# A new order for the second two thirds of a transformer block, and row-pass hops on four engines

## The chip, the cores and the metric

The kernel runs on one core of a Trainium2 chip. A core has five engines, each with its own instruction queue that it works off in order: TensorE (matmuls; PE in the profile, PEld for its weight loads), VectorE (DVE), ScalarE (ACT), GpSimd (POOL) and SyncE (SP, which here issues most DMAs). Engines wait for each other through semaphores. The metric is the time of one execution on the device in microseconds; lower is better.

## The reference

One block of a transformer with adaptive layer normalization, for 2048 tokens of width 448 (inputs and output bfloat16):

```python
mod = (silu(c) @ w_mod).reshape(1, 6, 1, 448)          # sa, ca, ga, sb, cb, gb
h = layernorm(x) * (1 + ca) + sa
x = x + ga * A(h, wqkv, wo)      # 16 heads of 28; each token attends to itself and
                                 # 7 tokens at steps of 2 behind it; softmax; @ wo
h = layernorm(x) * (1 + cb) + sb
x = x + gb * B(h, w1, b1, w2, b2)  # layernorm once more, @ w1 (448x1792) + b1, gelu (tanh), @ w2 + b2
```

## The kernel before

Even and odd tokens don't attend to each other, so the tokens are held as two sequences of 1024, and every tile carries both. The front (layer normalization, transposition, q, k and v) and the output side run in 8 tiles p = 0 to 7 of 128 positions of both sequences; attention runs in 9 batches i = 0 to 8 of 114 positions; the MLP runs in 4 tiles t = 0 to 3 of 256 positions. ScalarE's tables divide the whole into phases: attention batches 0 to 4, MLP tile 0, batches 5 and 6, tile 1, batches 7 and 8, tiles 2 and 3; a table load (`tbl`) stands between exp and gelu.

A batch is: v (`v5f`, `v5r`: a matmul over 128 rows and a rest over 64), the logits in two halves (`lt`, line 781), exp on ScalarE (line 788), the mask on VectorE (line 794), the sums `pd` (line 803) and the weighted values `po` (line 814), log and exp of the sums on ScalarE (lines 823 and 825), and their product on VectorE (`omul`, line 831). Then, for a tile, `wo` (line 851, or in two passes at line 575), and on VectorE the residual sum (`x1`, line 860), statistics (line 459), a normalization (line 481), two products with the modulation (`h2`, line 869), statistics and a normalization again, and the copy of a tail of 64 columns (lines 493 to 495); `rstd` between them is on GpSimd (line 472). A transposing DMA of SyncE (`yT`, line 884) brings the result into the layout for w1. An MLP tile is w1 (seven pairs of column blocks, line 575), 14 gelus on ScalarE (line 914), w2 (line 938, for the last tile line 956), and the residual sum (`fin`, line 962), which reads x plus a bias that GpSimd makes beforehand (`x1p`, line 891; a tiny copy `gate`, line 918, holds it back until the first gelu). The weights w2 are multiplied by a gate vector on VectorE (`w2_scale`, line 704, seven of them), after their loads (line 378). `windows` (lines 731 and 732) copies columns for v.

Where a matmul's inner dimension is cut to 64 rows, two of them run side by side in the upper and the lower half of the array, and write into two PSUM areas. In a first pass each half adds its share to its own area, in a second pass the halves change areas. The second pass must not begin before the first has ended, so between them stands a *hop*: an instruction on another engine that waits for the last matmul of the first pass and on which the first matmul of the second pass waits. `swapped` adds the hop, `paired` uses it for w1, for wo of tiles 4 to 7 and for v of batch 8, and the MLP uses it for w2 of tiles 0 to 6; there are 40. In TensorE's order other work stands between the two passes of a pair (`...p` and `...q`; for w2 `..._l` and `..._h`).

Nothing is scheduled at run time. The program makes a list of 781 tasks (`add`), each with an engine, an estimate of its time, a function that emits its instructions, and, for some, alternatives on other engines (`alt`). `ORDER` is the list of task numbers in which they are emitted; a letter behind a number picks an alternative (A ScalarE, D VectorE, P GpSimd, R another form on TensorE). An engine's queue is what stands in `ORDER` for it, in that order. `SLOTS` gives each buffer its place (PSUM has four of two banks); a task that writes a new buffer into a place waits for the last user of the one before. Both were written by a search outside the kernel.

Task numbers that are used below: 182 and 179 are the scalings of w2's blocks 4 and 1, 178, 183, 184 others of them; 352 and 385 are the omul of batches 3 and 4, 353 (`wo2`) and 386 (`wo3`) the output projections that need them; 463 and 500 are v of batches 5 and 6; 268 is yT0; 472, 473 and 509, 510 are pd and po of batches 5 and 6; 477, 479 and 514, 516 are the passes of wo4 and wo5, 515 the hop between the last two; 547, 549, 550 and 569 are passes of w1 in tile 1; 579 is the hop of w2 for tile 2; 535 and 498 are yT5 and yT4; 668 is the first task of w1 in tile 2; 629 is a copy of windows, 371 and 497 are tails.

Of the kernel before, what the change touches and what calls it, by code (L numbers as in the profile page):

```python
# [50 lines left out]
]  # L51
ORDER = """
3 14 17 0 1 15 5 9 10 18 11 16 13 19 20 2 6 24 21 73 55+12@55 26 12 71 25 56 72 74 57 75 22 58 77 23 59 60 27 62 61 76
32 4 67 66 68+11@68 78 63 28 108 64 30 110 69 79 84:A 89:P 31 65 70 109 111 80 88:P 83 34 81 112:P 87:A 29 101+9@101
85 90:A 93:P 36 114 94+3@94 82 95 113 102 92:A 91 115:D 86 103 116 96 120:A 144 97 99 104 106 117:A 135 98 118:A 142
105 119:A 145 143 133 100 146 121 136 134 137 126 148 107 147 149:D 127 7 138 122 150 124 129 139 190 198 123 191 200
140 128 141 199 269 125 236 271 130 270 207 40 209 33 241 237 201 38 208 210 185 211 35 242 39 202 154 153 151:A 152
187 8 238 239 212 159 203 213 186 204 214:D 155 240 205 215 188 278 156 279 280 160 206 307:R 161 281 243 282 272 192
273:A 37 157 189 171 162 308:D 194 172 193 283 244 218 163 195 219 275 173 284 196 216 167 158 285 217 246 462:P 197
164 286 168 165 228 169:D 174 274 276:D 309 277 312 220 313 166 310 314 221 229 225 230 224 311 222:D 247 315 170 245  # L60
176 317 316 175 248 233 226 232 290 318 227 249 289:A 319 287:A 43 288 320 234 250 223 592:P 593 46 321 45 253 345 47
342 346 251 594 231 303 499:P 252 324 343 322 291 44 254 595 323 325 347 326 344 292 304 255 327 293 348 328 373:R 256
305 294 329 257 350 258 375 378 52 330 376 340:R 53 333 379 235 377 334 331 374 296 300 295 332 259 41 335 351 380 299
336 341 49 337 260 297 382 262 381 301 263 261 349 264 338:A 352 463 383 339 265 384 353 266 267:D 406 385 268 500 354
# [8 lines left out]
580 598 635 532 533 638 636 581 534:D 639 535 602 582 588 498 604 605 641 640 603 642 587 606 643 607 667 589 678 608
644 668 609 669 583 679 670 610 645 613 680 646 611 681 684 612 614 615 685 647 682 590 674 683 648 703 691 686 649
687 671 650 617 675 651 698 672 616 692 460 618 673 453 619 688 652 622 677 653 620 676 693 689 699 655 623 690 654
696 621 656 700 624 694 657 708 705 695 701 658 697 715 660 702 659 661 662 709 663 664 625 665:A 626 716 710 666 627
# [26 lines left out]
class Plan:  # L103
# [53 lines left out]
def kernel(  # L157
# [14 lines left out]
    nc = tc.nc  # L172
# [3 lines left out]
    P = Plan()  # L176
    add = P.add
# [368 lines left out]
    def swapped(first, bufs, second):  # L546

        ends = []

        def hop():  # L550
            nop = nc.sync.nop()
# [484 lines left out]
```

## Time and profile before

| | |
|---|---|
| time, median of 3 runs | 171.2 us (170.81 to 173.26) |
| the profiled execution, as timed | 171.57 us |
| its span, first to last instruction | 169.9 us |
| mean granted TensorE clock | 0.998 |
| DMA | 18.84 MB, mean 111 GB/s |

The page gives the busy time of each engine and the costliest groups of instructions. A timeline row has the start in us from the span's start, the length in us, the engine, the line, the operation, out<-in with their shapes, the count, and in brackets idle time of the engine just before with what ended it. Successive matmuls overlap, so a row's length holds some 0.16 us of the last matmul's end, and a distance from start to start is the better measure. A row of stretches has the bounds and length in us, then the busy time of TensorE, its weight loads, VectorE, ScalarE and GpSimd with the count of instructions, the granted clock, the share of DMA time and GB/s. SPq is SyncE issuing a DMA; the landing comes later.

### The profile page before, as it was taken

The numbers are of one execution on the slowest core, as the hardware profiler recorded it, in microseconds if no ns is written. First come the engines' busy times: TensorE is split into PE (matmuls) and PEld (weight loads), VectorE is DVE, ScalarE is ACT, GpSimd is POOL, SyncE is SP. The second block draws the span as 40 slices with busy tenths as digits, with TensorE's granted clock in tenths as the row PEclk, the third lists the DMA queues.
The fourth block names the chain that finished last, engine by engine and source line by source line (L and its number), as shares of the span: only waits on it lengthen the run. The fifth ranks groups of instructions, "written<-read, shape, count | busy, mean of one in ns | idle before, by whom it ended". The sixth has DMA issues, their size and how long they took to land.

```text
span 169.9 us, 5815 instructions
## 1 busy us (share of the span) xinstructions
PE 160.9 (95%) x2528; PEld 86.8 (51%) x2528; DVE 118.3 (70%) x273; ACT 102.7 (60%) x142; POOL 47.1 (28%) x71
## 2 busy tenths in 40 slices
PE   7999999988999899999999999999799999999992
PEld 4678545444545544445555444556355555555650
DVE  6889799858899698698797459995559941300023
ACT  3378978697489944879447169948335920096300
POOL 3136422300351100391720014650010654007200
PEclk9999999999999999999999999999999999999999
DMA  5999989899999999910060000006013115100004
GB/s 155 319 355 293 193 242 158 168 127 173 227 183 262 174 136 256 139 30 4 8 121 4 4 0 0 4 4 123 5 58 123 39 21 106 54 4 0 0 17 149
DMA packets 35577, 18.84 MB, mean 111 GB/s; under 512 B 28507, under 2 KB 34592, under 8 KB 35552
## 3 DMA queue, kind: packets, MB, share of 16 engines
q1 hardware_dynamic: 35548, 18.47, 51.4%
q8 instruction: 20, 0.33, 0.9%
q14 instruction: 5, 0.04, 0.1%
q10 hardware_dynamic: 4, 0.00, 0.0%
HBM read 9.81 MB, written 1.84 MB: 69 GB/s over the span
## 4 chain that ended last, share of the span: by engine, by line
PE 64%; DMA 17%; DVE 10%; ACT 2%; POOL 2%; issue 2%; SPq 1%; DVEq 0%; POOLq 0%; ACTq 0%
PE p L575 25%; PE p L938 17%; DMA kT<-zy 6%; PE pw L851 4%; PE pq L591 4%; PE p L956 3%; PE pw L575 3%; DMA x_all<-in_A_x_dram 3%; DMA yT<-zy 3%; DVE stt L459 3%; DMA wm_st<-in_w_mod_dram 3%; DMA zT<-zy 2%; PE lt L781 2%; PE po L814 2%; POOL rs_all L472 1%
## 5 line engine op out<-in xcount | busy, mean ns | idle before, releaser
L914 ACT ACTIVATE hm<-p,b_col 128x512 bf16<-128x512 f32 x56 | 34.0, 692 | 28.1 <-PE p L575 28.1
L575 PE MATMUL p<-yT,w_s 64*128 64x512 bf16 x336 | 41.9, 376 | 1.1 <-DMA yT<-zy 1.1
L938 PE MATMUL p<-w_s,hm 64*128 64x448 bf16 x392 | 39.3, 350 | 0.0
L472 POOL TENSOR_TENSOR rs_all<-mvs,neg_half 128x2 f32<-128x2 f32 x22 | 16.9, 775 | 65.2 <-DVE mvs L461 65.0
L938 PEld LDWEIGHTS <-hm 64*128 64x128 bf16 x392 | 19.3, 94 | 16.4 <-issue 0.6
L575 PEld LDWEIGHTS <-w_s 64*128 64x128 bf16 x336 | 17.6, 94 | 19.4 <-issue 1.5
L962 DVE TENSOR_TENSOR x_all<-p,x1p 128x896 bf16<-128x896 f32 (+2 forms) x10 | 8.9, 900 | 24.2 <-PE p L956 16.6
L788 ACT ACTIVATE et<-lt 128x928 bf16<-128x928 f32 x18 | 16.2, 942 | 5.5 <-PE lt L781 5.3
L459 DVE BATCH_NORM_STATS2 stt<-x_all 128x6 f32<-128x448 bf16 x32 | 18.6, 611 | 0.8 <-DMA x_all<-in_A_x_dram 0.5
L891 POOL TENSOR_TENSOR x1p<-x_all,gbb_bc 128x448 f32<-128x448 bf16 x16 | 17.5, 1116 | 0.1
L591 PE MATMUL pq<-wqk_st,hT 128*128 128x448 bf16 x72 | 15.2, 354 | 0.3 <-DVE hT L505 0.3
L860 DVE TENSOR_TENSOR x_all<-pw,x_all 128x896 bf16<-128x896 f32 x8 | 8.7, 1088 | 7.0 <-PE pw L575 6.6
L794 DVE TENSOR_TENSOR et<-et,mask 128x928 bf16<-128x928 bf16 x18 | 11.7, 668 | 2.1 <-ACT et L788 2.1
L831 DVE TENSOR_TENSOR qT<-po,den 128x912 bf16<-128x912 f32 x9 | 9.9, 1098 | 3.4 <-PE po L814 1.8
L823 ACT ACTIVATE den<-pd 128x928 f32<-128x928 f32 x9 | 8.5, 942 | 5.1 <-PE pd L803 3.2
L575 PE MATMUL p<-yT,w_r 64*128 64x512 bf16 x56 | 10.8, 376 | 0.0
L671 ACT CAST zy<-pq 128x896 bf16<-128x896 f32 x10 | 8.9, 911 | 3.0 <-PE pq L597 1.4
L591 PEld LDWEIGHTS <-hT 128*128 128x128 bf16 x72 | 6.4, 98 | 7.4 <-issue 1.6
L869 DVE TENSOR_TENSOR h<-h,mod_bc 128x896 bf16<-128x896 bf16 x16 | 9.7, 613 | 0.2
L825 ACT ACTIVATE den<-den,den_bias 128x928 f32<-128x928 f32 x9 | 9.6, 1072 | 0.2
L481 DVE TENSOR_SCALAR h<-x_all,mvs,rs_all 128x448 bf16<-128x448 bf16 x16 | 8.0, 529 | 2.3 <-POOL rs_all L472 2.2
L459 DVE BATCH_NORM_STATS2 stt<-h 128x6 f32<-128x448 bf16 x16 | 9.5, 613 | 0.1
(121 smaller groups left out, 202.6 us busy)
## 6 DMA issues: line engine op xcount, KB each, us to landing
w_s<-in_B_w_dram SPq DMA_DIRECT2D x7, 224.0 KB, 6.3
out_dram<-x_all SPq DMA_DIRECT2D x7, 224.0 KB, 2.0
x_all<-in_A_x_dram SPq DMA_DIRECT2D x3, 448.0 KB, 5.2
wmod<-in_w_mod_dram SPq DMA_DIRECT2D x3, 448.0 KB
w_s<-in_B_w_dram SPq DMA_DIRECT2D x3, 448.0 KB
wqk_st<-in_A_wqkv_dram SPq DMA_DIRECT2D x3, 225.0 KB, 4.3
wm_st<-in_w_mod_dram SPq DMA_DIRECT2D x1, 672.0 KB, 4.6
x_all<-in_A_x_dram SPq DMA_DIRECT2D x2, 224.0 KB
```

The source lines that it names most:

```text
L459: add("DVE", 0.53, lambda: nc.vector.bn_stats(out=stt[:, w, b, 0:6], in_=src()), reads=reads, bufs=bufs, after=early if w == b == 0 else ( ...
L472: ways = {"POOL": (0.55 + 0.17 * n, lambda: nc.gpsimd.tensor_tensor(out=r, in0=v, in1=neg_half[:, 0:n], op=ALU.pow))}
L575: mm = nc.tensor.matmul(out(), lhsT=lhs(kt, rows), rhs=rhs(kt, rows), start=start and kt == 0, stop=not start and kt == n - 1, tile_positi ...
L591: nc.tensor.matmul(out(), lhsT=lhs(kt, slice(0, 128)), rhs=rhs(kt, slice(0, 128)), start=first and kt == 0, stop=not first and kt == KT - 2)
L788: exps.append(add("ACT", 0.83, lambda half=half, lt=lt: nc.scalar.activation(out=et.t[:, 2 * half:2 * half + 2].rearrange("p r m c -> p r ...
L794: nc.vector.tensor_tensor(out=ev, in0=ev, in1=mask[:], op=ALU.mult)
L825: exps.append(add("ACT", 0.96, lambda: nc.scalar.activation(out=den.t[:], in_=den.t[:], func=ACT.Exp, scale=-1.0, bias=den_bias[:]), bufs= ...
L831: nc.vector.tensor_tensor(out=qT[:, :, LEAD + q00:LEAD + q00 + 2 * WQ], in0=po.t[:, :, 0:NS * 4 * WQ].rearrange("p j (m c) -> p m j c", c=WQ),
L869: add("DVE", 0.55, lambda vec=vec, op=op: nc.vector.tensor_tensor(out=h2.t[:], in0=h2.t[:], in1=vec.unsqueeze(1).to_broadcast([128, NS, D] ...
L891: add("POOL", 1.0, lambda n=n: nc.gpsimd.tensor_tensor(out=x1p.t[:, n, :], in0=xn(p, n), in1=gbb2_bc[:], op=ALU.add), reads=[f"x{p}", "gbb ...
L914: gelus.append(add("ACT", 0.585, lambda f=f, a=a, p1=p1s[g]: nc.scalar.activation(out=hm.t[:, f].rearrange("p n c -> p (n c)"), in_=p1.t[: ...
L938: mm = nc.tensor.matmul(p2.t[:, n, 0:D], lhsT=hm.t[rows, f, n, q * 128:(q + 1) * 128], rhs=w2_s[rows, f, :], start=done == 0 and f == fs[0 ...
```

## The change

`SLOTS` and `ORDER` are replaced from the 109th entry of `ORDER` on; TensorE's own queue is the same up to its 81st task (po3). The search that wrote the new lists kept VectorE and GpSimd from running at the same time where both use the port that they share (tasks marked `port`). And a hop may now stand on GpSimd, ScalarE or VectorE, not only on SyncE; in the new order 29 of the 40 do (13 on ScalarE, 9 on GpSimd, 7 on VectorE). Two tails and a windows copy change engines: 371 from GpSimd to VectorE, 497 from ScalarE to GpSimd, 629 from VectorE to GpSimd.

```diff
 SLOTS = [
-    0, 0, 1, 1, 0, 0, 0, 0, 1, 2, 3, 0, 1, 0, 2, 3, 0, 2, 3, 2, 0, 1, 0, 0, 3, 1, 2, 1, 4, 2, 2, 1, 1, 2, 0, 3,
+    0, 0, 1, 1, 0, 0, 0, 0, 1, 2, 3, 0, 1, 0, 2, 3, 0, 2, 3, 2, 0, 1, 0, 0, 1, 1, 2, 3, 2, 0, 4, 1, 1, 2, 0, 3,
...
 ORDER = """
...
-336 341 49 337 260 297 382 262 381 301 263 261 349 264 338:A 352 463 383 339 265 384 353 266 267:D 406 385 268 500 354
-306 386 355 357 48 131 50 501 132 387 464 410 502 51 54 465 390 420 411 302 183 417 421 412 42 179 356 407 388 415 418
-391 182 416 422 408 298 389 358 409 392 425 427 426 359 414 419 360 413 361 430 393 424 178 442 437 362 423 431 177
...
+336 341 337 49 260 297 382 262 381 263 301 182 349 261 264 338:A 352 500 383 339 384 266 463 265 267:D 179 268 385 353
+306 386 354 48 50 131 464 132 387 501 51 410 465 54 388 406 417 302 389 420 502 418:D 411:D 355 42 357 419 421:A 358
...
-405 472 459 473 474 451 505 475 508 450 629 476 509 452 510 511 477 512 630 478 479 536 631 513 547 480 632 548 567
-481 633:D 514 482 549 515 568 569 550 571 570 516 551 554 540 517 553 552 541 483 542 484 485 537 545 486 556 557 487
...
+400 443 365 434 461 503 445 466 455 467 401 448 368 402 456 504 403 404:D 370 369 469 449:A 371:D 506 444 372 450 507
+446 470 405 458 471 468 457 505 508 472 459 451 474 475 509 452 510 473 511 630 476 512 567 631:P 513 477 632 478:A
+536 514 633:D 479 515:D 516 480 550 517 547 551 483 540 548 481 453 518 549 541 568 482 519 484 569 520 553 521 552
...
 """
...
-        def hop():
-            nop = nc.sync.nop()
+        def hop(e):
+            nop = e.nop()
             for mm in ends:
                 link(mm, nop)
             ends.append(nop)
 
         a = first(ends)
-        b = add("SP", 0.05, hop, needs=a, name="hop")
+        b = add("SP", 0.05, lambda: hop(nc.sync), needs=a, name="hop", alt={"POOL": (0.05, lambda: hop(nc.gpsimd)), "ACT": (0.05, lambda: hop(nc.scalar)),
+                                                                           "DVE": (0.05, lambda: hop(nc.vector))})
         return a + second(ends, [b])
```

More of the change, by code (lines that the diff above doesn't have):

```diff
@@ L55 @@
 85 90:A 93:P 36 114 94+3@94 82 95 113 102 92:A 91 115:D 86 103 116 96 120:A 144 97 99 104 106 117:A 135 98 118:A 142
[L56 to L59, printed above, removed]
@@ L60 @@
-164 286 168 165 228 169:D 174 274 276:D 309 277 312 220 313 166 310 314 221 229 225 230 224 311 222:D 247 315 170 245
-176 317 316 175 248 233 226 232 290 318 227 249 289:A 319 287:A 43 288 320 234 250 223 592:P 593 46 321 45 253 345 47
-342 346 251 594 231 303 499:P 252 324 343 322 291 44 254 595 323 325 347 326 344 292 304 255 327 293 348 328 373:R 256
-305 294 329 257 350 258 375 378 52 330 376 340:R 53 333 379 235 377 334 331 374 296 300 295 332 259 41 335 351 380 299
-336 341 49 337 260 297 382 262 381 301 263 261 349 264 338:A 352 463 383 339 265 384 353 266 267:D 406 385 268 500 354
[3 rows of a table removed]
@@ L68 @@
-398 367 455 399 504 400 401 467 448 368 369 506 449 456 469 507 402 457 370 403 470 371 468 445 372 458 471 443 404:D
-405 472 459 473 474 451 505 475 508 450 629 476 509 452 510 511 477 512 630 478 479 536 631 513 547 480 632 548 567
-481 633:D 514 482 549 515 568 569 550 571 570 516 551 554 540 517 553 552 541 483 542 484 485 537 545 486 556 557 487
-538 518 555 520 539 558 546 519 488 560 543 489 544 559 572 521 561 492 522 562 493 563 574 523 577 524 566 525 573
-564 490 565 584 491 526 494 591 529 575 530 527 596 528 599 495 576 597 496 578 600 531 585 579 497:A 601 637 586 634
@@ L73 @@
[L73 to L76, printed above, removed]
[3 rows of a table removed]
+105 119:A 145 143 133 100 146 121 136 134 126 137 148 107 147 149:D 7 138 127 150 122 124 139 129 190 198 123 191 200
@@ new lines @@
+140 128 141 199 269 125 271 236 270 130 207 40 209 33 241 201 237 208 38 210 185 211 35 242 39 202 154 153 151:A 152
+187 212 238 203 159 239 213 204 214:D 8 215 186 155 188 205 240 206 156 160 278 307:R 161 279 280 37 281 243 162 171
+282 272 192 273:A 157 189 308:D 194 172 193 244 173 283 163 195 218 158 219 275 196 284 167 216 217 246 197 285 462:P
+164 286 168 165 228 169:D 174 274 309 312 276:D 277 220 313 310 314 166 221 229 225 230 224 311 222:D 247 315 245 176
+170 317 316 175 248 233 232 226 290 318 227 249 289:A 319 287:A 234 43 288 320 250 223 592:P 593 46 321 45 253 345 47
@@ new lines @@
+342 346 251 594 231 303 499:P 252 324 343 322 291 44 254 595 323 325 347 326 344 292 304 255 327 293 348 328 373:R 256
+305 329 294 257 350 258 375 378 52 330 376 340:R 333 53 379 235 377 334 331 374 296 300 332 295 259 41 351 335 380 299
+336 341 337 49 260 297 382 262 381 263 301 182 349 261 264 338:A 352 500 383 339 384 266 463 265 267:D 179 268 385 353
+306 386 354 48 50 131 464 132 387 501 51 410 465 54 388 406 417 302 389 420 502 418:D 411:D 355 42 357 419 421:A 358
+356 390 422 359 424 407 361 426 360 362 425 412 408 363 423 409 184 415 437 391 178 416 392 430 414 438 298 394 413
@@ new lines @@
+181 427 393 431:D 395 439 428:P 180 432 183 429 396 435 454 397 177 436 398 366 440 399 442 441 629:P 447 364 433 367
+400 443 365 434 461 503 445 466 455 467 401 448 368 402 456 504 403 404:D 370 369 469 449:A 371:D 506 444 372 450 507
+446 470 405 458 471 468 457 505 508 472 459 451 474 475 509 452 510 473 511 630 476 512 567 631:P 513 477 632 478:A
+536 514 633:D 479 515:D 516 480 550 517 547 551 483 540 548 481 453 518 549 541 568 482 519 484 569 520 553 521 552
+554 522 542 570 485 524 537 571 487 555 486 560 523 538:A 556 488 539 545 525 561:P 526 546 557 527 543 562 489 558:P
@@ new lines @@
+544 529 559 572 576 528 490 584 564 530 492 573 563 566 577 531 565 575 591 596 599 585 600 597 601 578 493 586:A 598
+637 491 532 634 494 638 533 588 496 635 579:D 495 587 534:D 639 535 636 497 574 498 602 589 581 604 605 603 640 641
+606 642 580 643 607 667 644 668 582 608:A 609 669:A 645 610 698 646:A 611 670 647 674 671 675 648 703 706 699:A 700
+672 612 649 704 673 701 651 678 613 677 650 676 614 681 679:D 652 615 688 653 616 682:A 655 683 617 689:A 702 618 680
+686 654 656 691 687 619 685 690 620 692 684 693 657 695 658 715 697 660 696 622 708 694 661 623 621 659 624 662 626
@@ L80 @@
+709 664 625 663 716 710:P 627 665:A 705 666 712 717:P 707 628 718 711 719 713 722 720 732 723:A 745 733:P 734 746:P
+735 739 738 747 736 583 724 721 751 590 725 750 460 729 737 726:D 728 727 757 742 761 730 731 752 743:A 740 744 741
+753 714 754 762 756 748 749 773 755 777 763 778 764:P 759 765 779 760 758 766 769 767 774 770 775 776 768 771 780 772
 """
```

14 rows, old and new, of tables (ORDER, SLOTS) are left out of this document.

## The prediction

> **What bounds the kernel now.** I read the page first, then the busy time by stretches, then the timelines of the stretches in which TensorE is not busy.
>
> ```profile
> span 169.9 us, 5815 instructions
> ## 1 busy us (share of the span) xinstructions
> PE 160.9 (95%) x2528; PEld 86.8 (51%) x2528; DVE 118.3 (70%) x273; ACT 102.7 (60%) x142; POOL 47.1 (28%) x71
> ```
>
> TensorE is the bound: 160.9 of 169.9 us. The change adds and removes no matmul, so it can only move what TensorE loses between matmuls. TensorE's own order is the same up to the tasks that follow po3, at 58.3 us. From there the stretches are (first the length, then TensorE's busy time):
>
> ```profile
> 58.00:64.60 6.60, 6.40 (x79) 3.21 (x68) 6.02 (x13) 3.23 (x3) 0.69 (x1) 1.00 1.10 154
> 84.70:91.00 6.30, 5.87 (x184) 3.25 (x184) 5.84 (x8) 3.35 (x4) 1.33 (x1) 1.00 0.44 86
> 119.00:121.20 2.20, 1.14 (x14) 0.38 (x12) 1.95 (x3) 1.56 (x2) 0.00 (x0) 1.00 0.01 1
> 64.60:84.70 20.10, 20.10 (x312) 9.76 (x309) 16.86 (x36) 15.04 (x21) 9.18 (x11) 1.00 0.49 82
> 91.00:119.00 28.00, 28.00 (x522) 14.28 (x518) 21.28 (x39) 19.29 (x26) 7.54 (x9) 1.00 0.11 21
> 121.20:166.50 45.30, 45.30 (x430) 25.05 (x430) 16.87 (x36) 17.27 (x29) 11.75 (x15) 1.00 0.16 46
> ```
>
> The granted clock is 1.00 in all of them. TensorE stands idle 0.20, 0.43 and 1.06 us in the first three and not at all in the last three. So there are three places to gain in, and 93.4 us in which a new order can only do harm. The 3.4 us behind 166.5 are the last residual sum and its store, which stay in their order.
>
> **58 to 66 us: two scalings of w2 move forward on VectorE.** TensorE before, in order v5, wo2, v6, wo3, the b1 transpose, two row remainders, then w1:
>
> ```profile
> 58.34 1.31 PE L591 MATMUL pv<-Wv,hw 128*128 128x448 bf16 x6
> 59.85 1.69 PE L851 MATMUL pw<-wo_s,qT 128*128 128x448 bf16 x8 [0.20 <-DVE qT L831]
> 61.37 1.30 PE L591 MATMUL pv<-Wv,hw 128*128 128x448 bf16 x6
> 62.51 1.68 PE L851 MATMUL pw<-wo_s,qT 128*128 128x448 bf16 x8
> 64.11 0.18 PE L712 MATMUL pb<-ident,b_rows 14*128 14x14 bf16 x1
> 64.22 0.55 PE L597 MATMUL pv<-Wv,hw 64*128 64x448 bf16 x4
> 64.61 0.59 PE L575 MATMUL p<-yT,w_s 64*128 64x512 bf16 x4
> ```
>
> ```profile
> 58.73 1.06 DVE L831 TENSOR_TENSOR qT<-po,den 128x912 bf16<-128x912 f32 x1
> 59.71 0.69 DVE L481 TENSOR_SCALAR zy<-h,mvs,rs_all 128x448 bf16<-128x448 bf16 x2
> 60.43 0.20 DVE L494 COPY zy<-zy 128x128 bf16<-128x128 bf16 x1
> 60.54 1.10 DVE L831 TENSOR_TENSOR qT<-po,den 128x912 bf16<-128x912 f32 x1
> ```
>
> The new order is v6, v5, wo2, wo3, and on VectorE scaling 182 stands ahead of the first omul (352) and scaling 179 ahead of the second (385). Task v5 takes the PSUM slot that omul 352 empties; wo3 reads what omul 385 writes. The scaling's own row, and its load's:
>
> ```profile
> L704 DVE TENSOR_TENSOR w_s<-w_s,mod_bc x7: 582/612/1455, 66.1 to 77.3; 128x896 bf16<-128x896 bf16 x7
> ```
>
> ```profile
> 56.02 0.38 SPq L378 DMA_DIRECT2D w_s<-in_B_w_dram  x1
> ```
>
> ```profile
> w_s<-in_B_w_dram SPq DMA_DIRECT2D x7, 224.0 KB, 6.3
> ```
>
> Step by step, with 0.58 us for a scaling. Omul 352 ends at 58.73 + 1.06 + 0.58 = 60.37. TensorE has v6 behind it by then (58.34 + 1.14, the start to start distance from 61.37 to 62.51) and waits; v5 runs to 61.51 and wo2 (1.60, from 62.51 to 64.11) to 63.11. VectorE does two normalizations and the tail (0.75 from the end of one omul to the start of the next) up to 61.12 and meets scaling 179. That reads the part of w2 whose load SyncE issues at 56.02, and the order of SyncE's queue up to there is unchanged; 6.3 us to landing puts it at 62.3. So VectorE stands still for 1.2 us, the scaling ends at 62.9, omul 385 at 64.0, wo3 at 65.6, and w1 starts 0.50 later (64.11 to 64.61) at 66.1 instead of 64.61: **+1.5**. If the load has landed by 61.1, omul 385 ends at 62.80, wo3 isn't held up, and w1 starts at 65.21: +0.6. Those are the two bounds. I take 1.5, since the landing in that row was recorded for this very load. The transposing DMA behind the tail (yT0) also goes out some 0.6 us later; that is hidden, since w1 itself comes later by as much.
>
> **84 to 91 us: the port.** VectorE and GpSimd before:
>
> ```profile
> 83.60 2.43 POOL L891 TENSOR_TENSOR x1p<-x_all,gbb_bc 128x448 f32<-128x448 bf16 x2
> ```
>
> ```profile
> 83.73 1.40 DVE L794 TENSOR_TENSOR et<-et,mask 128x928 bf16<-128x928 bf16 x1 [0.24 <-ACT et L788]
> 85.05 1.03 DVE L494 COPY zy<-zy 128x128 bf16<-128x128 bf16 x1
> ```
>
> The tail copy took 0.20 at 60.43 and takes 1.03 here, ending as GpSimd's second x1p does (83.60 + 2.43 = 86.03): the two engines take turns, and a meeting costs VectorE up to 0.83. What that does to TensorE, and beside it the same kind of work without such a wait:
>
> ```profile
> 84.80 0.77 PE L803 MATMUL pd<-et,ones_k 64*32 64x464 bf16 x8
> 85.20 0.90 PE L814 MATMUL po<-et,vb 64*32 64x57 bf16 x64
> 86.03 2.82 PE L938 MATMUL p<-w_s,hm 64*128 64x448 bf16 x28
> 88.79 0.39 PE L803 MATMUL pd<-et,ones_k 64*32 64x464 bf16 x8
> 89.59 0.67 PE L814 MATMUL po<-et,vb 64*32 64x57 bf16 x64 [0.42 <-DVE qT L831]
> 90.20 0.93 PE L575 MATMUL pw<-wo_s,qT 64*128 64x448 bf16 x8
> ```
>
> ```profile
> 116.28 0.67 PE L814 MATMUL po<-et,vb 64*32 64x57 bf16 x64
> 116.77 0.42 PE L803 MATMUL pd<-et,ones_k 64*32 64x464 bf16 x8
> 116.97 0.73 PE L814 MATMUL po<-et,vb 64*32 64x57 bf16 x64
> ```
>
> A pd and a po need 0.69 (116.28 to 116.97). Here they took 1.23 (84.80 to 86.03) and 1.41 (88.79 to 90.20): 1.26 us too much, of which only 0.43 is visible as idle. The new order moves the windows copy (629) from VectorE to GpSimd and sets it with two x1p behind the first gelus, the other two x1p later; it puts three tasks instead of two between the logits and pd5, and sets pd6, po6 and po5 one after the other. At best all 1.26 goes. At worst one meeting of 0.83 is left on VectorE ahead of the residual sum whose PSUM slot pd6 takes; my walk through the order leaves VectorE some 0.2 us there, so 0.63 comes back and 0.63 is gained. I take the middle, **-0.95**.
>
> **119 to 121 us: the transposed activations for w1 of tile 2.**
>
> ```profile
> 116.09 4.93 DMA yT<-zy
> 121.03 0.14 issue
> 121.16 1.90 PE p L575 x16
> ```
>
> TensorE is ready at 120.1 and waits 1.06 us for the second of two transposing DMAs, issued at 116.09. With the terms above it will be ready at 120.1 + 1.5 - 0.95 = 120.65, so the DMA must be issued 0.4 us earlier than before for the wait to go. In TensorE's new order four w1 half passes fewer (28 matmuls at 1.90/16 = 0.12 us, 3.3 us) stand ahead of wo5's second pass, from which VectorE's chain to that DMA starts; 0.55 of that is lost to the terms above, and hop 579, which now stands on VectorE ahead of the normalization of that chain and waits there for a half of w2 (16 + 12 matmuls), may take up to 1 us. Some 1.7 us are left where 0.4 are needed. The chain also held this pair, where two normalizations that took 0.69 at 59.71 took 2.12 beside an x1p:
>
> ```profile
> 105.25 2.12 DVE L481 TENSOR_SCALAR h<-x_all,mvs,rs_all 128x448 bf16<-128x448 bf16 x2
> ```
>
> So the wait goes: **-1.06** (bounds 0 and -1.06). What is late next is VectorE's omul ahead of wo6, with under 1 us to spare.
>
> **The hops.** A hop is one instruction that waits for the end of a first row pass and releases the second:
>
> ```profile
> L551 SPq EVENT_SEMAPHORE  x40: 17/17/17, 65.7 to 160.5; - x40
> ```
>
> 29 of the 40 leave SyncE: 13 to ScalarE, 9 to GpSimd, 7 to VectorE. On SyncE nothing waited for them in TensorE's rows, so nothing is won there; the stretches at 64.6, 91 and 121.2 have no idle time. Elsewhere a hop costs its 17 ns and its place: it comes late by what is ahead of it (at most 1.10, the longest VectorE row above), and what is behind it waits for the first pass. The cover is the other half pass that TensorE has in between, 6 matmuls or more (0.7 us), and all that it waits for is computed ahead: I find no hop that is late in my walk, with the least room (some 0.15 us) at wo6 behind ScalarE's table load. Cost taken: 0, bounds 0 and 1.10 each. The other moves (two tails between engines, four more scalings, stores that SyncE issues earlier or later, the gelus' order) have slack of a microsecond or more: 0.
>
> **Sum.** +1.5 - 0.95 - 1.06 = -0.5 us. The profiled execution took 171.57 us for its span of 169.9, so 171.1; it lay 0.37 above the median of the three runs, so against the median of 171.2 I say **170.7 us**.
>
> **Rivals.**
> First, the load is there in time: +0.6 in place of +1.5, and the time is 171.2 + 0.6 - 0.95 - 1.06 = 169.8; with all of the 1.26 it is 169.5, and with no cost at all 168.9. For it: other loads of that queue may land sooner than the one recorded. Against: the DMA share is 1.10 in that stretch, so the queues are full.
> Second, the exclusion exists in the list only. Each engine keeps its own order, but nothing makes x1p wait until VectorE's copies are through; as soon as VectorE is 1.5 us late out of the first stretch, they meet again, and the 1.26 stays: 171.2 + 1.5 - 1.06 = 171.6. [...]
> Third, and slower: VectorE doesn't catch up at all, and the chain to yT4 starts no earlier. Then the 1.06 stays too: 171.2 + 1.5 = 172.7. It decides when VectorE's tail ahead of that DMA is done less than 0.4 us earlier than before. For it: VectorE is busy 5.84 of 6.30 us from 84.7 on; against: the 3.3 us of w1 that no longer stand ahead.
> Fourth, slower by over 2%: hops on computing engines come late in four or more places, at 1.10 each: 170.7 + 4.4 = 175.1. For it: 29 places, several tight. Against: a late hop on one engine delays TensorE, which lets the others catch up. [...] No row here shows a hop on a computing engine.
>
> **Chances.** Forecast 0.43, first rival 0.24, second 0.14, third 0.12, fourth 0.07. The range goes from 168.9 (the first rival's end) to 172.9 (the third with 0.2 to spare) and leaves out the fourth and the edges. About 2% (3.4 us) is what a measurement tells from no change. Faster than that, under 167.8, needs more than all that TensorE loses from 58 us on (0.20 + 1.26 + 1.06 = 2.5): 0.04, out of the first rival. Slower, over 174.6: 0.07. Within: 0.89.
>
> **What would show it.** After the change: a scaling (line 704) ahead of VectorE's second omul with a wait on w_s's DMA near 62.3, and w1's first matmul near 66; if that is at 65.2 or less, the first term is wrong. No DVE copy or normalization of 1 us or more between 82 and 90, and pd and po at about 0.7 us; otherwise the second is. No wait of w1 for yT after 115. TensorE waiting for ACT, DVE or POOL at a second pass of line 575 or 938 would be a late hop, and would sink the forecast.

## The result, and the profile after

| | median | lowest to highest | runs |
|---|---|---|---|
| before | 171.94 us | 170.61 to 174.12 | 20 |
| after | 173.04 us | 171.55 to 176.09 | 20 |

The ratio after to before is 1.0068, with a 95% interval of 1.0039 to 1.0097: the change makes the kernel 0.7% slower, some 1.2 us. That is inside 2%, but it is a loss, and the forecast was a gain of 0.5 us. The ratio leaves out the longest executions of either kernel, here and below, so it can differ from that of the medians.

The profiled execution happens to be the longest of the twenty (176.09 us). Its page:

```profile
span 174.3 us, 5821 instructions
...
PE 162.9 (93%) x2528; PEld 85.6 (49%) x2528; DVE 118.6 (68%) x273; ACT 101.8 (58%) x141; POOL 47.2 (27%) x72
...
PEclk9999999699999999999699999999999999999999
```

TensorE is busy 162.9 us instead of 160.9 with the same matmuls, and in two of the forty slices its clock is down to 0.6. Among the costliest groups there is one wait that was not there before:

```profile
L939 PE MATMUL p<-w_s,hm 64*128 64x448 bf16 x392 | 40.6, 357 | 2.5 <-DVE w_s L705 2.5
```

That is w2's matmul, waiting 2.5 us for a scaling of w2 on VectorE (lines of the changed kernel are one higher than before's). Its place, in the timeline of all engines:

```profile
75.35 0.62 DVE L705 TENSOR_TENSOR w_s<-w_s,mod_bc 128x896 bf16<-128x896 bf16 x1
75.88 1.22 DVE L481 TENSOR_SCALAR h<-x_all,mvs,rs_all 128x448 bf16<-128x448 bf16 x1
75.94 1.03 POOL L701 TENSOR_TENSOR gbb_bc<-mod_bc,b_bc 128x448 f32<-128x448 bf16 x1 [0.94 <-PE p L576]
76.91 0.24 POOL L919 COPY seen<-hm 128x1 bf16<-128x1 bf16 x1
77.08 1.03 POOL L733 COPY hw<-hT 128x1024 bf16<-128x1024 bf16 x1
77.13 1.46 DVE L870 TENSOR_TENSOR h<-h,mod_bc 128x896 bf16<-128x896 bf16 x1
77.47 1.49 PE L939 MATMUL p<-w_s,hm 64*128 64x448 bf16 x14
78.08 2.79 POOL L892 TENSOR_TENSOR x1p<-x_all,gbb_bc 128x448 f32<-128x448 bf16 x2
78.52 2.83 DVE L705 TENSOR_TENSOR w_s<-w_s,mod_bc 128x896 bf16<-128x896 bf16 x2
81.28 0.61 DVE L870 TENSOR_TENSOR h<-h,mod_bc 128x896 bf16<-128x896 bf16 x1
81.41 2.29 PE L939 MATMUL p<-w_s,hm 64*128 64x448 bf16 x18 [2.45 <-DVE w_s L705]
```

GpSimd runs four tasks and the tiny gate back to back, from 75.94 to 80.87 (the product `gbb2`, the gate, the windows copy 629, two x1p). Beside it, VectorE's normalization takes 1.22 instead of 0.40 (75.03), its product with the modulation 1.46 instead of 0.61 (81.28), and the two scalings 2.83 together, where one alone takes 0.62 at 75.35. The kernel marks all these tasks `port`. That the two engines share a port there is not shown by any run; the rows show the lengths, and those are what is used below. The two scalings are 180 and 183. Scaling 183 stood early in the old order, ahead of 417; the new one put it behind 180, and block 10 of w2, the eighth that the first pass of w2 uses, hangs on it. So TensorE stops after 14 matmuls and stands idle 2.45 us. What the clock does just after, by stretches of 3.41 us (TensorE's busy time is the second figure, the clock comes before the DMA share):

```profile
28.12:31.53 3.41, 1.56 (x76) 0.79 (x50) 2.01 (x6) 2.20 (x3) 0.00 (x0) 1.00 0.70 146
31.53:34.94 3.41, 3.41 (x11) 1.36 (x9) 2.13 (x5) 2.05 (x3) 1.39 (x2) 0.50 0.68 132
79.32:82.73 3.41, 1.32 (x15) 0.79 (x16) 3.34 (x6) 2.56 (x4) 1.55 (x2) 1.00 0.00 0
82.73:86.14 3.41, 3.41 (x80) 1.73 (x78) 2.63 (x10) 1.39 (x2) 1.56 (x3) 0.50 0.02 5
86.14:89.55 3.41, 3.41 (x96) 1.90 (x94) 2.43 (x4) 1.41 (x3) 1.79 (x2) 1.00 0.03 5
```

Twice a stretch in which TensorE is busy less than half of 3.41 us (1.56 and 1.32) is followed by one of the same length with a granted clock of 0.50, which by my estimate (half of 3.41) does 1.7 us less work. The first lies ahead of the changed part, behind a wait of 1.71 us at a pd (30.28) that has no wait in the profile of the kernel before (28.00); the second follows the new wait. Whether such a wait brings the half clock is tested below.

Lengths of five stretches, from TensorE's rows: from the first matmul of po4 to that of w1 (tile 0), of w2 (tile 0), of wo6, of w1 (tile 3), to TensorE's end, and from there to the end of the span.

```
                             po4    w1_0   w2_0   wo6    w1_3   rest
before                       8.57  10.67  43.90  25.42  21.91  3.35
before, hops moved           7.50  10.67  44.02  24.91  21.91  3.40
before, 183 behind 180       7.50  10.67  43.81  25.10  21.91  3.36
after                        7.48  10.67  47.04  24.20  21.90  3.70
after, profiled again        7.89  10.67  45.51  24.20  21.90  3.69
after, 183 ahead of hop 418  7.48  10.67  44.16  24.20  21.90  3.70
after, GpSimd's block later  7.79  10.66  43.89  24.20  21.90  3.70
after, three moves           7.74  10.67  42.95  24.19  21.90  3.61
```

The first stretch differs by up to 1 us between executions of the same order. The loss lies in the third, a gain in the fourth, a small loss at the end.

### The profile page after: what moved, and what is told of

Its sections match the earlier page's. It is cut to its first block, busy times and chain, and to the rows that moved or that the text cites. A ratio compares the mean times of both kernels' runs of the same rounds, so it can differ in the third digit from the quotient of the medians.

```text
span 174.3 us, 5821 instructions
## 1 busy us (share of the span) xinstructions
PE 162.9 (93%) x2528; PEld 85.6 (49%) x2528; DVE 118.6 (68%) x273; ACT 101.8 (58%) x141; POOL 47.2 (27%) x72
## 4 chain that ended last, share of the span: by engine, by line
PE 72%; DMA 8%; DVE 8%; SPq 3%; ACT 3%; POOL 3%; issue 1%; DVEq 0%; ACTq 0%; POOLq 0%
PE p L939 22%; PE p L576 19%; PE pq L592 8%; DMA zT<-zy 5%; PE pw L852 3%; PE pw L576 3%; DMA x_all<-in_A_x_dram 3%; PE p L957 3%; PE lt L782 3%; PE po L815 3%; DVE w_s L705 2%; POOL rs_all L472 2%; PE pv L750 2%; DVE stt L459 2%; DVE h L870 2%; PE pq L598 1%
## 5 line engine op out<-in xcount | busy, mean ns | idle before, releaser
L939 PE MATMUL p<-w_s,hm 64*128 64x448 bf16 x392 | 40.6, 357 | 2.5 <-DVE w_s L705 2.5
L939 PEld LDWEIGHTS <-hm 64*128 64x128 bf16 x392 | 18.8, 95 | 20.5 <-issue 4.4
L576 PEld LDWEIGHTS <-w_s 64*128 64x128 bf16 x336 | 16.6, 94 | 19.4 <-DVE x_all L861 0.4
L892 POOL TENSOR_TENSOR x1p<-x_all,gbb_bc 128x448 f32<-128x448 bf16 x16 | 17.0, 1083 | 6.6 <-PE p L939 6.6
L592 PE MATMUL pq<-wqk_st,hT 128*128 128x448 bf16 x72 | 16.8, 383 | 0.2 <-ACT hT L507 0.2
L795 DVE TENSOR_TENSOR et<-et,mask 128x928 bf16<-128x928 bf16 x18 | 10.8, 630 | 6.6 <-ACT et L789 6.5
L592 PEld LDWEIGHTS <-hT 128*128 128x128 bf16 x72 | 6.9, 104 | 8.3 <-issue 3.5
L870 DVE TENSOR_TENSOR h<-h,mod_bc 128x896 bf16<-128x896 bf16 x16 | 10.5, 670 | 0.2
L765 ACT CAST vb<-pv 128x896 bf16<-128x896 f32 x7 | 6.4, 908 | 4.5 <-PE pv L598 4.3
```

What stands on the lines that cost most here:

```text
L576: mm = nc.tensor.matmul(out(), lhsT=lhs(kt, rows), rhs=rhs(kt, rows), start=start and kt == 0, stop=not start and kt == n - 1, tile_positi ...
L592: nc.tensor.matmul(out(), lhsT=lhs(kt, slice(0, 128)), rhs=rhs(kt, slice(0, 128)), start=first and kt == 0, stop=not first and kt == KT - 2)
L795: nc.vector.tensor_tensor(out=ev, in0=ev, in1=mask[:], op=ALU.mult)
L870: add("DVE", 0.55, lambda vec=vec, op=op: nc.vector.tensor_tensor(out=h2.t[:], in0=h2.t[:], in1=vec.unsqueeze(1).to_broadcast([128, NS, D] ...
L892: add("POOL", 1.0, lambda n=n: nc.gpsimd.tensor_tensor(out=x1p.t[:, n, :], in0=xn(p, n), in1=gbb2_bc[:], op=ALU.add), reads=[f"x{p}", "gbb ...
L939: mm = nc.tensor.matmul(p2.t[:, n, 0:D], lhsT=hm.t[rows, f, n, q * 128:(q + 1) * 128], rhs=w2_s[rows, f, :], start=done == 0 and f == fs[0 ...
```

## The experiments

Theory: the loss is the wait of w2 for scaling 183, made by its new place and GpSimd's block beside it. Rivals: the hops on computing engines are late, or the place alone, or GpSimd's block alone, is to blame. A second question came up on the way: what the half clock has to do with it.

**The changed kernel once more**, for a profile without the disturbance at 31 us.

> The changed kernel itself once more, beside the next two on one chip. Theory A: TensorE waits about 2.4 us for scaling 183 at w2's first pass again, in a profile without the disturbance ahead of 58 us too, and the clock is halved for 3.4 us behind it; 1 to 2.5 us above the kernel before and 1.5 to 3 us above the version with 183 early. If the wait was one execution's accident: none in this profile, and a time within 0.6 us of the kernel before.

173.1 us (171.04 to 174.92, 6 runs) against 171.64; ratio 1.0114, interval 1.0042 to 1.0185. The profiled execution took 171.04, with the same wait and no half clock:

```profile
74.03 1.49 PE L939 MATMUL p<-w_s,hm 64*128 64x448 bf16 x14
77.96 1.88 PE L939 MATMUL p<-w_s,hm 64*128 64x448 bf16 x18 [2.45 <-DVE w_s L705]
```

So the wait belongs to the order. The half clock does not follow it every time.

**Scaling 183 back to an early place**, and nothing else (the lines of `ORDER` are shown in part, here and below, with `...` for what lies between):

```diff
-302 389 420 502 418:D 411:D ... 428:P 180 432 183 429
+302 389 420 502 183 418:D 411:D ... 428:P 180 432 429
```

> The changed kernel with one task moved: scaling 183 of w2 goes ahead of hop 418 on VectorE, some 9 us earlier. Theory A (w2's first pass waits 2.45 us for this scaling, which GpSimd's copies and sums hold up at the shared port, and TensorE's clock is halved for 3.4 us right behind the wait): the wait falls below 0.5 us, the half clock behind it goes, and the time is 2.5 to 4 us below the changed kernel's 173.0, so 169 to 170.5, below the kernel before. Theory B (the hops on computing engines are what costs): the time stays within 1 us of 173.0. Theory C (VectorE is late as a whole, the wait only moves to scaling 180 or a later one): a wait of 1.5 us or more remains at line 939, and the time stays above 172.

171.04 us (169.21 to 172.49, 12 runs) against 171.51; ratio 1.002, interval 0.996 to 1.0081. The loss is gone, but the gain that was expected in its place did not come:

```profile
75.09 3.19 PE L939 MATMUL p<-w_s,hm 64*128 64x448 bf16 x32
...
86.93 0.39 PE L804 MATMUL pd<-et,ones_k 64*32 64x464 bf16 x8 [0.74 <-DVE et L795]
87.26 1.31 PE L939 MATMUL p<-w_s,hm 64*128 64x448 bf16 x12
88.94 0.39 PE L804 MATMUL pd<-et,ones_k 64*32 64x464 bf16 x8 [0.38 <-DVE x_all L963]
```

All 32 matmuls of w2's first two passes run through. Some ten us later pd5 waits 0.74 for VectorE's mask and pd6 0.38 for its residual sum: once TensorE is not held up at w2, it meets a VectorE that is late. That its meetings with GpSimd make it late is my reading here; the three moves below bear it out.

**GpSimd's block later.** The gate of tile 0 reads the gelu block 11 instead of block 0, and gate, windows and the first x1p (443) stand behind 434:

```diff
-399 442 441 629:P 447 364 433 367 400 443 365 434 461
+399 441 447 364 433 367 400 365 434 442 629:P 443 461
```

> The changed kernel with GpSimd's gate of tile 0 hung on the 12th gelu in place of the first, so that gate, windows copy and two x1p start some 4 us later; VectorE's order is unchanged. Theory A, as to the port: with only gbb2 left beside them, scalings 180 and 183 take 0.6 us each instead of 2.83 together, the wait at w2 falls from 2.45 to at most 1 us, and the time is 1.5 to 3.5 us below 173.0. If the place of 183 in VectorE's list is enough by itself (theory C), the wait stays above 1.8 us and the time within 0.7 us of 173.0.

171.01 us (169.7 to 173.4, 12 runs); ratio 0.9985, interval 0.9943 to 1.0028. Scaling 183 keeps its late place here:

```profile
75.22 3.29 PE L940 MATMUL p<-w_s,hm 64*128 64x448 bf16 x32
75.43 1.15 DVE L705 TENSOR_TENSOR w_s<-w_s,mod_bc 128x896 bf16<-128x896 bf16 x2
78.42 0.19 POOL L920 COPY seen<-hm 128x1 bf16<-128x1 bf16 x1 [3.70 <-ACT hm L915]
```

With GpSimd idle beside them the two scalings take 1.15 instead of 2.83, and the wait is gone. So, in the new order, it took both, the late place and GpSimd's work beside it.

**The old order with 183 late** was meant as the other half of that:

```diff
-411 302 183 417 421 ... 395 441 180 436 447
+411 302 417 421 ... 395 441 180 183 436 447
```

> The kernel before with scaling 183 moved behind scaling 180 on VectorE, where the changed kernel has it. Theory A: w2's first pass waits for it 1 to 2 us, and if a wait of that length is what halves the clock, 3.4 us at half clock follow; 1 to 3.5 us above the kernel before. Otherwise, if it takes the rest of the new order to make the loss: within 0.6 us of the kernel before.

171.57 us (170.33 to 172.75, 12 runs); ratio 0.9997, interval 0.9958 to 1.0036. Here the two scalings took 1.15 at 77.25, GpSimd being done at 76.85, and w2 ran through. But this run doesn't test the new place. In the old order `w2_1_l0` (454), the first pass of w2, is emitted ahead of the moved scaling, so that it doesn't wait for it and takes block 10 unscaled: its eighth pair of matmuls runs at 77.16 (75.83 and seven pairs of 0.19), and scaling 183, the second of the two, begins at 77.79. Only `w2_0_l0` waits for it, 16 matmuls later. That the late place costs nothing without GpSimd's work rests on the run before this one.

**The hops.** First the old order with its 40 hops on the engines that the new order gives them (29 not on SyncE), then the new order with all hops on SyncE.

> The kernel before with one part of the change alone: the same 29 hops stand on ScalarE, GpSimd and VectorE, each at its place in the old order. Theory A: a hop costs its place in a queue and little more; the time is within 0.6 us of the kernel before. Theory B: 1 us or more above it, with waits of TensorE for those engines at second passes.

> The changed kernel with all 40 hops back on SyncE, in the same order. Theory A: hops cost little; the one on GpSimd that holds gbb2 back for 0.9 us is gone, so GpSimd's work and the meetings come up to 0.9 us earlier, the wait at w2 is 1 to 2.5 us, and the time lies 0 to 1 us below the changed kernel's. Theory B: the time falls by more than 1.2 us and waits at second passes vanish.

The old order with moved hops: 171.95 us (169.62 to 173.54, 12 runs), ratio 1.0007, interval 0.995 to 1.0063. The hops cost nothing that can be measured. The new order with all hops on SyncE: 172.11 us (169.91 to 175.05, 12 runs), ratio 0.9988, interval 0.9942 to 1.0034; by this ratio the loss is gone, which is more than I had expected; by the medians (172.11 against 171.64) 0.5 us of it is left. Its rows:

```profile
72.03 1.03 POOL L701 TENSOR_TENSOR gbb_bc<-mod_bc,b_bc 128x448 f32<-128x448 bf16 x1
...
76.06 1.99 DVE L705 TENSOR_TENSOR w_s<-w_s,mod_bc 128x896 bf16<-128x896 bf16 x2
78.10 1.88 PE L939 MATMUL p<-w_s,hm 64*128 64x448 bf16 x18 [1.44 <-DVE w_s L705]
```

The wait is 1.44 instead of 2.45, for two reasons. In the changed kernel hop 428 on GpSimd waits 0.94 us for a first pass of TensorE, and `gbb2` behind it starts that much later (the bracket at 75.94 above). Without it GpSimd's block starts earlier, another normalization meets it, but one of the two scalings escapes: from that normalization to the end of scaling 183 VectorE takes 5.95 us (72.10 to 78.05), against 6.32 in the second profile of the changed kernel (71.59 to 77.91). And two hops on VectorE (418 and 411) hold VectorE in the changed kernel, which they don't on SyncE:

```profile
69.03 1.15 DVE L459 BATCH_NORM_STATS2 stt<-x_all 128x6 f32<-128x448 bf16 x2 [0.46 <-PE p L576]
```

Counted from the first matmul of w1, VectorE comes to that normalization 0.57 us earlier. What these hops cost is what was queued behind them. The meetings themselves are there with either place of the hops.

**Three moves together**: 183 early; GpSimd in the order `gbb2`, windows, gate (on gelu block 13), three x1p and, behind `rstd`, the fourth, so that its products fall where VectorE has little of that kind and more statistics (three of those took 1.63 us beside the gate and the windows copy with GpSimd's block later, and 1.64 with GpSimd idle in the second profile of the changed kernel); the store of tile 6 right behind its sum (767, 768).

```diff
-302 389 420 502 418:D 411:D ... 180 432 183 429
+302 389 420 502 183 418:D 411:D ... 180 432 429
-397 177 436 398 366 440 399 442 441 629:P ... 445 466 ... 506 444 372
+397 177 629:P 436 398 366 440 399 441 442 ... 445 444 466 ... 506 372
-769 767 774 770 775 776 768 771
+769 767 768 774 770 775 776 771
```

> The changed kernel with three moves: scaling 183 ahead of hop 418 as before; gate of tile 0 on its 14th gelu and three of the four x1p behind it, under VectorE's statistics, which don't meet GpSimd; the store of tile 6 ahead of one that waits for a later sum. Theory A: no wait for scalings, the waits of pd5 and pd6 (0.74 and 0.38 us with 183 early alone) fall to 0.4 us together, the time from TensorE's end to the span's end falls by 0.3 us; 1 to 2 us below the kernel before, and the fastest so far. If something else sets the pace between 78 and 119 us, the waits stay and the time is within 0.7 us of the kernel before.

169.4 us (168.29 to 171.43, 6 runs) against 171.64; ratio 0.9884, interval 0.9826 to 0.9943. Faster than both kernels, if by less than 2%. Run once more on another chip:

> The three moves once more, on whatever chip comes, for a narrower interval. If the gain is real: 169 to 170 against 171.5 to 172 of the kernel before, ratio 0.984 to 0.994, and a mean granted clock of 0.99 or less in no more than 2 of 12 runs. If the six runs were lucky: 170.5 to 171.5, ratio 0.994 to 1.

169.33 us (168.81 to 172.17, 10 runs) against 171.1; ratio 0.9922, interval 0.9882 to 0.9962. In the table above, which has the first of the two runs, the third stretch is 42.95, with no wait of pd or w2; the store's move gave only 0.09 of the 0.3 lost at the end.

**Does the wait bring the half clock?** I take a mean granted clock of 0.99 or less as the mark of an execution with at least one episode (1.7 us in 170 are 1%), wherever in it the episode lies; the first profile of the changed kernel, with two, has 0.980, and the second, with none, 0.997. They are 15 of 20 and 3 of 6 runs of the changed kernel, against 9 of 84 of the kernel before in the experiments. To separate the wait from the new order, the old order (183 late) got a wait made by hand: VectorE reads a block of w2 into statistics that nobody uses, ahead of scaling 183.

```diff
 def scale(e, i=i):
+    if i == 5:
+        for _ in range(5):
+            e.bn_stats(out=idle_out[:], in_=w2_s[:, 10, :])
+        e.bn_stats(out=idle_out[:], in_=w2_s[:, 10, 0:128])
     e.tensor_tensor(out=w2_s[:, 2 * i:2 * i + 2, :], ...
```

> The order of before with scaling 183 behind scaling 180, and ahead of scaling 183 VectorE reads one block of w2 into statistics that nobody uses, five times whole (0.55 us each) and once 128 columns (0.2 us): 2.95 us more work on VectorE, so that TensorE, which had some 0.4 us to spare there, waits about 2.5 us ahead of the last block of w2's first pass, as it does in the changed kernel (2.45). Theory (the wait itself brings TensorE's clock down to half for one 3.41 us episode in most executions, and the new order has nothing else to do with it): at least 6 of 12 runs have a mean granted clock of 0.99 or less, against about 1 in 10 of the kernel before, and the time is 171.6 + about 2 + about 1.2 = 174.5 to 175. Rival (the episodes belong to the new order or to other waits, and a wait of 2.5 us costs its own length): 0 to 2 of 12 runs at 0.99 or less, and 173.5 to 174.

> As the run before, with nine whole reads ahead of scaling 183 (4.95 us), so that TensorE waits about 4.5 us there. Theory (the longer the wait, the more surely the half clock follows): nearly all of 12 runs have a mean granted clock of 0.99 or less; 171.6 + about 4 + 1.7 = 177 to 178. Rival (no link with the wait): 0 to 2 of 12 runs, and 175.5 to 176.

In both, `w2_1_l0` takes block 10 unscaled, as above, and the wait lies ahead of the last block of `w2_0_l0`. The shorter: 173.99 us (171.06 to 178.12, 10 runs) against 172.06, ratio 1.005, interval 0.9982 to 1.0117, and 7 of 10 runs at 0.99 or less. Its profiled execution is one of the other three: clock 1.00, and a wait of 1.70, less than aimed at. There the two scalings and the product ahead of the reads met no work of GpSimd (1.16 at 72.25, 0.61 at 74.38); in the profile of the longer run they did (1.99 and 1.39), so by my estimate from these rows other executions of the shorter may have waited up to 1.6 us longer. The stretch of 3.41 us in which most of the 1.70 lies (how its bounds are found is told in the last section):

```profile
76.24:79.65 3.41, 1.88 (x20) 0.87 (x17) 3.17 (x6) 2.73 (x4) 1.19 (x2) 1.00 0.00 0
```

The longer (nine reads): 177.84 us (4 runs) against 172.06, ratio 1.0379, interval 1.0318 to 1.044, and all 4 at 0.981 or less. Its wait and its stretches:

```profile
83.92 0.56 PE L942 MATMUL p<-w_s,hm 64*128 64x448 bf16 x2 [5.64 <-DVE w_s L708]
```

```profile
77.45:80.86 3.41, 0.83 (x10) 0.29 (x7) 3.24 (x6) 1.67 (x2) 0.00 (x0) 1.00 0.00 0
80.86:84.27 3.41, 0.35 (x2) 0.10 (x1) 3.20 (x6) 0.00 (x0) 0.00 (x0) 0.50 0.00 0
84.27:87.68 3.41, 3.41 (x80) 1.88 (x80) 1.87 (x8) 1.78 (x2) 1.36 (x2) 0.50 0.03 7
87.68:91.09 3.41, 3.41 (x96) 1.90 (x94) 1.75 (x5) 1.70 (x2) 2.45 (x3) 1.00 0.09 20
```

Two stretches in a row with little work (0.83 and 0.35), and two at half clock, each one behind.

Then the same in the new order, first with the three moves (four reads and a short one), and, as that went to another place than meant, with GpSimd's block later (four reads):

> The changed kernel with the three moves (169.4), and ahead of scaling 183 four whole reads of a block of w2 and one of 128 columns on VectorE (2.4 us), so that TensorE waits about 2.4 us ahead of the same block as in the changed kernel. Theory (the wait brings the half clock): 6 or more of 12 runs at a mean granted clock of 0.99 or less, and 169.4 + about 2.2 + about 1.2 = 172.5 to 173.3, about the changed kernel's own 173. Rival (the three moves removed something else that brought it): 0 to 2 of 12 runs, and 171.5 to 172.

171.65 us (169.71 to 174.54, 10 runs) against 172.06, ratio 0.9969, interval 0.9916 to 1.0023; 2 of 10 runs at 0.99 or less. This was a miss of mine: with the three moves scaling 183 stands early, so the reads stood there too, and w2's pass waited only 0.71, for another scaling. They did show something else:

```profile
65.90 2.57 DVE L708 BATCH_NORM_STATS2 idle_out<-w_s 128x6 f32<-128x448 bf16 x4
68.51 0.29 DVE L709 BATCH_NORM_STATS2 idle_out<-w_s 128x6 f32<-128x128 bf16 x1
...
68.93 2.12 PE L577 MATMUL p<-yT,w_s 64*128 64x512 bf16 x18 [1.87 <-DVEq L552]
```

A hop on VectorE (line 552) stood behind the reads, and TensorE waited 1.87 us for it.

> The changed order with GpSimd's block later (no port meeting at the two scalings, 171.0), scaling 183 in its late place, and ahead of it four whole reads of a block of w2 by VectorE (2.57 us for four where they were seen): TensorE waits about 2.4 us in w2's first pass, as in the changed kernel, but with no port meeting. Theory (the loss is the wait, whatever makes it, and the wait brings the half clock in most executions): 6 or more of 12 runs at a mean granted clock of 0.99 or less, 171.0 + about 1.5 + about 1.2 = 173 to 174.5, as slow as the changed kernel or slower. Rival (the port meeting itself, or the changed kernel's execution in other places, brings the half clock): 0 to 2 of 12 runs, and 172 to 172.8.

174.26 us (173.74 to 176.84, 4 runs) against 171.1, ratio 1.0181, interval 1.0097 to 1.0265; all 4 at 0.99 or less. The reads pushed scaling 183 into GpSimd's later block (it took 1.45), so the wait was 3.40, longer than meant, and not free of a meeting with GpSimd:

```profile
80.85 1.45 DVE L709 TENSOR_TENSOR w_s<-w_s,mod_bc 128x896 bf16<-128x896 bf16 x1
81.79 2.79 POOL L896 TENSOR_TENSOR x1p<-x_all,gbb_bc 128x448 f32<-128x448 bf16 x2
82.35 3.27 PE L944 MATMUL p<-w_s,hm 64*128 64x448 bf16 x18 [3.40 <-DVE w_s L709]
```

Put together, with the wait at w2 as profiled and the share of runs at 0.99 or less: no wait of this kind, 9 of 84 (before), 1 of 12 (its hops moved), 1 of 12 (183 early), 2 of 12 (GpSimd later), 1 of 12 (old order, 183 late), 2 of 16 (three moves); 0.71, with 1.87 earlier at a hop, 2 of 10; 1.44 us, 2 of 12; 2.45, 18 of 26; 3.40, 4 of 4; 5.64, 4 of 4. The shorter wait by hand had 7 of 10, with waits that differ between executions. A wait put by hand into the old order brought the half clock (4 of 4 with 5.64 us), and with the wait taken out of the new order 1 and 2 of 12 runs had it. So the wait is the cause. The new order with its other meetings didn't bring it without the wait (183 early, 1 of 12). Why the 1.87 us at the hop did so little is open.

## Why the prediction was wrong

The sum was +1.5 - 0.95 - 1.06 = -0.5, and the change cost 1.2 us instead. Of the 2.3 us between the forecast of 170.7 and the median of 173.04, 0.7 are the baseline: the kernel before, 171.2 in 3 runs, has a median of 171.94 in 20. The third rival's 172.7 comes nearest to the measured time, by luck: it rests on a wait for the transposing DMA that did go. What the runs show for each term:

**The two scalings ahead of the omuls, +1.5: it was nothing.** The order was read rightly, the wait for the load did not come. In the changed kernel:

```profile
60.05 0.58 DVE L705 TENSOR_TENSOR w_s<-w_s,mod_bc 128x896 bf16<-128x896 bf16 x1
...
60.68 2.66 PE L592 MATMUL pv<-Wv,hw 128*128 128x448 bf16 x12
...
62.75 0.62 DVE L705 TENSOR_TENSOR w_s<-w_s,mod_bc 128x896 bf16<-128x896 bf16 x1
63.18 3.19 PE L852 MATMUL pw<-wo_s,qT 128*128 128x448 bf16 x16
...
66.80 0.81 PE L576 MATMUL p<-yT,w_s 64*128 64x512 bf16 x6
```

```profile
w_s<-in_B_w_dram SPq DMA_DIRECT2D x7, 224.0 KB, 4.3
```

Both scalings start without a wait, v and wo run through, and w1 starts 6.12 us after v (60.68 to 66.80), where before took 6.27 (58.34 to 64.61) and I had 7.8. The step that failed in this term is "I take 1.5, since the landing in that row was recorded for this very load". The row was read rightly, but it tells of one execution: in the changed kernel the same load lands 4.2 us after its issue instead of 6.3, and SyncE issues it 3.52 us ahead of v (57.16 against 60.68) instead of 2.32 (56.02 against 58.34). So it lands at 61.4, and the scaling that needs it starts at 62.75. The rival that the load is there in time was right about this term. Even its +0.6 was too much, since scaling 182 ran before the omul was ready.

**84 to 91 us, -0.95: right in size in the changed kernel, by luck.** Its second profile:

```profile
87.68 0.39 PE L804 MATMUL pd<-et,ones_k 64*32 64x464 bf16 x8
88.00 1.31 PE L939 MATMUL p<-w_s,hm 64*128 64x448 bf16 x12
89.24 0.39 PE L804 MATMUL pd<-et,ones_k 64*32 64x464 bf16 x8
89.45 1.26 PE L815 MATMUL po<-et,vb 64*32 64x57 bf16 x128
```

No wait is left, though the meetings are: beside two x1p of GpSimd (82.45 to 84.49) VectorE's tail copy takes 0.94 at 82.60 and a normalization 1.16 at 83.47, where the prediction's sign was none of 1 us or more between 82 and 90. The third stretch less the 2.45 of w2 is 45.51 - 2.45 = 43.06, against 43.91, the mean of the three profiles of the old order: -0.85. But TensorE came 2.45 us late to this place, so VectorE had that much more time. Where it came on time (183 early) waits of 0.74 and 0.38 took the place of the old ones, and the stretch was 44.16. The gain came in the new order only with GpSimd's block where the three moves have it (42.95, or -0.96); in the later place tried before, both pd waited 0.38 and the stretch was 43.89.

**The transposed activations, -1.06: right.** The second transposing DMA is issued 4.36 us ahead of wo6 (115.18 against 119.54 in the second profile) instead of 3.09 (116.09 against 119.18), and TensorE runs from wo6 into w1 of tile 2 without a wait:

```profile
119.54 0.92 PE L576 MATMUL pw<-wo_s,qT 64*128 64x448 bf16 x8
120.30 0.81 PE L576 MATMUL p<-yT,w_s 64*128 64x512 bf16 x6
```

The old order's three profiles have that stretch at 25.42, 24.91 and 25.10, the new order's at 24.20 each time: -0.94 in the mean.

**"The other moves ... have slack of a microsecond or more: 0": here the prediction failed.** "Four more scalings" was one phrase of that sentence, and scaling 183 is one of the four. The sentence shows no sum, and it has no price for a meeting at the new place. There VectorE's queue holds four operations that the kernel marks `port`, and GpSimd's holds four beside them (1.03 to 1.40 each). The normalization took 1.22 instead of 0.40, the product 1.46 instead of 0.61, and the two scalings 2.83 instead of 1.15: 0.82 to 0.85 more for each of the four. VectorE came some 3.4 us later, which used up a slack of about 0.95 and left 2.45. So the slack was nearly what the sentence says; what it left out is the price of the meetings. I had the price of a meeting in hand (up to 0.83, from the tail copy), and used it for one stretch only, although the row of the scalings in the prediction has one of 1455 ns where the others take about 600. The second rival said that the exclusion exists in the list only, and in that it was right: nothing at run time held GpSimd's block off (75.94 to 80.87, beside VectorE's four from 75.88 to 81.35). But I let that rival lose the old gain of 1.26 at 84 us, not make a new meeting at 75. How far the list's estimated times were off is not settled: hop 428 moved GpSimd by 0.94, but with all hops on SyncE the two meet as well, with a wait of 1.44.

**The clock at 1.00: the price that was missing.** The prediction read a granted clock of 1.00 in all stretches and priced a wait at its own length. An episode costs 1.7 us more by my estimate (half of its 3.41; the third stretch took 47.04 with one and 45.51 without), and 18 of 26 runs had one, against 9 of 84 of the kernel before: 1.7 x (0.69 - 0.11) = 1.0 us in the mean. Together: +2.45 for the wait, +1.0 for the clock, -0.85 and -0.94 for the two gains, +0.3 at the end make +2.0, against a measured 1.2 (interval 0.7 to 1.7) and, with the second set of runs, 2.0 (0.7 to 3.2). The first interval doesn't reach the sum; the 0.8 us between are open.

**The hops, 0: right in the old order** (1.0007); in the new one they lengthen the wait at w2 from 1.44 to 2.45, through what stands behind them. The fourth rival's late hop was seen once: TensorE waited 1.87 us for a hop on VectorE, with 2.9 us of work ahead of it. That is more than the 1.10 that the prediction called the longest VectorE row (its own rows have 1.40 at 83.73). No profile of the new order without such reads shows TensorE waiting for a hop.

**The tail, 0: wrong by 0.3** in the four profiles of the new order that the table shows without the three moves. The last sum and its stores keep their order among themselves; moving the store of tile 6 gave back 0.09. But the profiles of the new order with all hops on SyncE, and with reads and GpSimd's block later, have 3.43, close to the old order's 3.35 to 3.40, so it may differ between executions. The rest is open.

## What to carry to other kernels

A task that moves needs its slack counted with the price of its new neighbours on the other engine, not with the length it has alone. Two static queues that a list keeps apart by estimated times had nothing here that kept them apart at run time (two scalings took 2.83 us instead of 1.15); a hop on one of them was enough to move it by 0.94 us. A wait of TensorE cost more than its length here: at 1.44 us the half clock came in 2 of 12 runs, at 2.45 us in 18 of 26, by my estimate with 1.7 us more each time. And a latency that decides a term should be taken from several executions: one landing of 6.3 us, which was 4.2 in the next, made the largest term of this sum.

## What the runs showed of the hardware that I had not expected

In the profiled execution of the changed kernel the two stretches at half clock begin at 31.53 and 82.73 us, 51.20 us apart; each lasts 3.41, and 51.2 is fifteen times 3.413. In the profile with four reads and GpSimd's block later they begin at 31.47 and 82.67, again 51.20 apart. The granted clock also fell to half behind the last matmul: in the profile of the kernel before, whose last matmuls are over at 166.53, it is 1.00 from 166.60 to 169.20 and 0.50 from 169.30 to the end. From that fall I estimated bounds for executions without an episode, in steps of 3.413. In the second profile of the changed kernel (mean clock 0.997) the clock falls at 168.15, and 27 steps ahead of that lies 75.99. The bounds of 76.24 and 79.65 for the shorter wait by hand are an estimate of the same kind.

TensorE's busy time in the stretch before did not decide it alone. Stretches with 1.56, 1.32, 1.31, 0.83, 0.35 and 0.32 were each followed by half clock. The one with 1.88 (the shorter wait by hand) was not, and the profiles with a wait of 1.44 at w2 (all hops on SyncE) and of 1.87 at a hop (three moves with reads) have a mean clock of 1.000 and 0.999, so no episode. But neither was one with 1.44 busy followed by it, around the same wait of 2.45:

```profile
75.99:79.40 3.41, 1.44 (x16) 0.90 (x17) 3.34 (x6) 2.46 (x4) 1.43 (x2) 1.00 0.00 0
79.40:82.81 3.41, 3.41 (x98) 1.71 (x93) 2.63 (x9) 1.78 (x2) 1.68 (x3) 1.00 0.02 5
```

So these runs show no single limit, since 1.56 was followed and 1.44 was not. What else counts is open, and with it the share of executions that a wait of a given length should hit. The two profiles with the wait of 2.45 differ in where an estimated bound cuts it: 2.09 us of it lay in one stretch where the half clock followed, 1.97 where it didn't. Whether that made the difference is not shown.

In none of these stretches was TensorE idle throughout: 1.85 us of idle time (3.41 - 1.56) came ahead of half clock, and 1.97 (3.41 - 1.44) in another did not.
